# Two-level gates from the fourth token group on, with the sums of the gate weights made one group earlier

## The chip, the cores and the metric

The kernel runs on one core of one Trainium2 chip. The metric is the device time of one execution in microseconds. The kernel before took 752.95 us, the median of three runs between 752.68 and 754.04 us. Engines are called by the profile's names: PE is TensorE (PEld its weight loads), DVE is VectorE, ACT is ScalarE, POOL is GpSimd, and SP issues most DMAs.

## The reference

The computation is a linear attention followed by a multiplicative feed-forward block, all in 32-bit floats. There are 8 batches, 8 heads, 576 positions and head size 64, so 4608 tokens of width 512; the inner width is 1024.

```python
kv = np.einsum('bhsd,bhse->bhde', k, v)
out = np.einsum('bhsd,bhde->bhse', q, kv)
rms = np.sqrt(np.mean(out * out, axis=-1, keepdims=True) + 1e-06)
attn = out / rms * g_norm
x = attn.transpose(0, 2, 1, 3).reshape(4608, 512)
a = x @ w1
b = x @ w2
return ((a * b) @ w3) @ w_out
```

## The kernel before

**Stages.** The kernel first multiplies w3 by w_out once (lines 1288 to 1376). Then it works through nine groups of 512 tokens in the order T = 0 to 6, 8, 7. Groups 0 to 7 are the first 512 positions of each batch; group 8 holds the 64 left-over positions of all batches. "The third group" is T = 2, "the fourth" is T = 3. A group has two parts: the gates, which compute a * b, and the projection with the folded weights (`project`, for T = 0, or `project_twice`).

**One-level gates.** `gates(T, p, ...)` handles row block p of four. It calls `winograd` (line 692), a Strassen-Winograd scheme of seven products in place of eight. A product is four fp32 matmuls of a 128x128 weight block against 256 token columns; the profile counts two instructions for each. PSUM results of the products a11, s1, s2 and s3 are copied to SBUF by ACT under the names p1, p5, u2 and u3 (`keep`, line 712); a piece c21 is copied at line 834. The third product adds into p1's PSUM bank, so PE cannot start it before the copy p1 is done; the fourth stands in the same way behind p5. DVE adds the parts and multiplies the two halves (lines 836 to 840). Twice in each block `winograd` calls `between()`: after u2 and after c11. That runs a step of `steps(T + 1)`, the attention of the next batch.

**Two-level gates.** Groups in IN_TWO, before the change T = 4, 5, 6, 8 and 7, do block 2 first, then blocks 0 and 1 together in `gates_of_two` (line 925), then block 3. `gates_of_two` applies the scheme a second time inside each of the seven products: twice 49 products of 128x128 against 128 columns (line 953), 196 instructions in the profile's count. It needs inner sums of the activations (`sum_x`, lines 918 to 921, eight DVE subtractions at the group's start) and of the weights.

**Weight sums.** `prepare_w` (line 870) is a generator of seven pieces, one for each outer product. A piece is three DVE instructions of 128x256 (lines 875 to 877) and three stores to the DRAM tile w_l2, or six for the products s1, s2 and s4, whose plain blocks are stored too. `replace_a21` (line 884) replaces seven blocks in place and stores three of them. Before the change three pieces are made in T = 2 (one behind each of the blocks 0 to 2) and four in T = 3 (two behind each of the blocks 0 and 1); `replace_a21` runs in block 2 of T = 3, at its first `between()`. The stored blocks come back in five DMAs by `load_w`: three in the projection of the group before the two-level group, the others within its gates.

**Turning by DMA.** q and the normed attention output x must be transposed. `turn_by_dma` (line 280) does that in three steps: a copy that separates the 16-bit halves (lines 297 and 299), a transposing DMA on SP (line 301), and a copy that joins the halves (line 311). For batches up to 4 (prepared in groups up to T = 3) POOL makes the copies; batch 1 is an exception, for which ACT makes most of them. For batches over FIRST_OF_TWO (5 on) `turns_by_scalar` (line 526) puts ACT's copies into slots. A slot is a key (stage, name): when `keep` or another copy with that name has been issued in that stage, `run_slot` traces the slot's calls, with an edge that holds them behind that copy on ACT. `begin` makes the first copy and the DMA, `end` the copy back. Keys such as (0, 3) belong to `gates_of_two` (half, product), ("p3", "u2") to a one-level block, and ("proj", "u2") to the projection.

**Order of work.** PE, POOL and SP run in the order in which the program is traced. DVE and ACT are ordered by the compiler's scheduler, except for stretches set by hand (DVE from block 3 on through the projection). `tc.issue_after(x)` adds an edge that keeps what is traced inside it behind x on x's own engine. SP therefore issues every store, load and transpose in traced order; one that waits holds all behind it. The trace has DVE waiting in order too, whatever the order is that the scheduler chose.

**PSUM.** Five banks serve the products (`ps_mm`), three the attention (`ps_at`).

Of the kernel before, what the change touches and what calls it, by code (L numbers as in the profile page):

```python
# [22 lines left out]
def kernel(  # L23
# [38 lines left out]
    DF = w1.shape[1]  # L62
    NP = H // 2
    KF = DF // P
    FIRST_OF_TWO = 4
    NH = KF // 2
    J = 4
    G = J * P
# [15 lines left out]
    def bank(pool, tag):  # L84
        return pool.tile([P, 512], FP32, name=tag, tag=tag)


    loaded, copies, adds = {}, {}, {}
# [166 lines left out]
    def all_of(steps):  # L255
        for _ in steps:
            pass
# [63 lines left out]
    def attention(b):  # L321
# [56 lines left out]
        def norm(o_ps, dsts):  # L378
# [3 lines left out]
            for i in range(n):  # L382
                sq = work.tile([P, G], FP32, name=f"sq{0 if b > FIRST_OF_TWO else i}", bufs=1)[:, 0:w]
                nc.scalar.activation(sq, o_ps[i], AF.Square)  # L384
# [41 lines left out]
        def product_left():  # L426

            xn = st["left"] = work.tile([P, NP, 2, D], FP32, name="xn_left", bufs=1)

            o_ps = [bank(ps_at, "at"), bank(*((ps_at, "at") if b > FIRST_OF_TWO else (ps_mm, "mm")))]  # L430
            for r in range(NP):
# [82 lines left out]
    def batch(b):  # L514
        if b not in batches:
            batches[b] = attention(b)
        return batches[b]

    slots, stage = {}, [None]
# [6 lines left out]
    def turns_by_scalar(b):  # L526

        a, turning = batch(b), {}

        def at(key, *call):  # L530
            slots.setdefault(key, []).append(call)

        def begin(name, f, *args):
            turning[name] = f(*args, nc.scalar.copy)
            next(turning[name])
            if name[0] == "q":
                next(turning[name])
            elif name[2]:
                for r in range(2):
                    next(turning["x", name[1], r])  # L540

        def end(name):
            all_of(turning[name])
            if name[0] == "q" and name[1] != "left":
                batch(name[1]).load_ahead("q", name[2])

        for r in (2, 3):
            at((0, 0), begin, ("q", b, r), a.q_by_dma, r)
        if b % 2:
            at(("p2", "c21"), begin, ("q", "left"), a.q_left_by_dma)  # L550
            at((0, 3), end, ("q", "left"))
        at((0, 6), end, ("q", b, 2))
        at((1, 0), end, ("q", b, 3))
        for h, begins, ends in (
            (0, ((0, 3), (0, 3)), ((1, 3), (1, 3))),
            (1, (("p3", "p1"), ("p3", "p5")), (("p3", "c21"), ("proj", "p1"))),
        ):
            for r in range(2):
                at(begins[r], begin, ("x", h, r), a.x_part_by_dma, h, r)
                at(ends[r], end, ("x", h, r))  # L560
        if b + 1 < B:
            n = batch(b + 1)
            for r in range(2):
                at(("p3", "u2"), begin, ("q", b + 1, r), n.q_by_dma, r)
                at(("proj", ("u2", "u3")[r]), end, ("q", b + 1, r))

    def steps(b):

        a = batch(b)
        a.start()
        more = b + 1 < B
        fs, ends = ([[] for _ in range(8)] for _ in range(2))

        def turn(i, f, *args, next_group=False):

            t = []

            def begin():
                t.append(f(*args))
                next(t[0])
                next(t[0])

            fs[i].append((begin,))
            (to_end if next_group else ends[i + 1]).append((lambda: all_of(t[0]),))

        if to_end:

            ends[0] += [(lambda: nc.gpsimd.tensor_copy(tick, late["p5"][:, 0, 0:1]),), *to_end]
        to_end.clear()
        odd = b % 2
        by_scalar = b > FIRST_OF_TWO
        if b == 1:
            early.extend(a.q_two_by_dma(r) for r in (0, 1))
            q_first = list(early)
            fs[0].append((a.begin_kv, 0, 1))

            def end_first():  # L600
                for t in q_first:
                    with tc.issue_after(copies["kv"].ins):
                        next(t)
                    all_of(t)

            ends[1].append((end_first,))
        fs[1] += [(a.begin_kv, 2, 3), (a.finish, 0)]
        if b == 1:
            last = {}

            def begin(name, behind, f, *args):
                last[name] = f(*args)
                with tc.issue_after(copies[behind][-1].ins):
                    next(last[name])
                next(last[name])

            def end(name, behind):
                with tc.issue_after(copies[behind][-1].ins):
                    next(last[name], None)
                all_of(last[name])  # L620

            fs[2] += [(begin, f"q{r}", "u2", a.q_two_by_dma, r) for r in (2, 3)]
            fs[3] += [
                (begin, "x", "u3", a.x_by_dma, 0, nc.scalar.copy),
                (begin, "left", "u3", a.q_left_by_dma),
            ]
            ends[4] += [(end, "q2", "p1"), (end, "q3", "p5"), (end, "x", "u2")]
            ends[5].append((end, "left", "u3"))
        elif by_scalar:
            turns_by_scalar(b)  # L630
        else:
            turn(1, a.q_two_by_dma, 2, 3)
            turn(2, a.x_by_dma, 0)
            if odd:
                turn(1, a.q_left_by_dma)
        second = 5 if b == 1 else 4
        if more:
            fs[second].append((batch(b + 1).begin_kv, 0, 1))
        fs[second].append((a.finish, 1))
        if odd:  # L640
            fs[3 if by_scalar else second].append((a.product_left,))
        if b == 1:
            turn(6, a.x_by_dma, 1)
            turn(7, a.x_left_by_dma, next_group=True)
        else:
            if not by_scalar:
                turn(5, a.x_by_dma, 1)
            if odd:
                turn(5, a.x_left_by_dma, next_group=more)
        if more and not by_scalar:  # L650
            turn(7 if b == 1 else 5, batch(b + 1).q_two_by_dma, 0, 1, next_group=True)
        if more:
            fs[7 if odd else 0].append((load_q_left, b + 1))
        return iter([lambda s=e + f: [f(*args) for f, *args in s] for e, f in zip(ends, fs)])
# [229 lines left out]
    def replace_a21():  # L884
        for n, (name, _) in enumerate(PRODUCTS):
            a11, _, a21, _ = w_blocks(name)
            nc.vector.tensor_sub(a21, a11, a21)
            if (0, n, "s3") in BLOCKS:
                store_w(n, "s3", a21)
# [387 lines left out]
    TWICE = (B, B - 1)  # L1277
    IN_TWO = (*range(FIRST_OF_TWO, B - 1), *TWICE)

# [8 lines left out]
    with tc.manual_schedule(  # L1288
# [6 lines left out]
        for e in range(2):  # L1295
            nc.scalar.dma_start(
                out=g_row[:, e * D:(e + 1) * D], in_=g_norm.rearrange("(o d) -> o d", o=1)
# [85 lines left out]
    for n, T in enumerate(groups):  # L1383
        pieces = steps(T + 1) if n + 2 < NG else iter([])

        def between():
            if len(converted) < len(begun):
                with tc.issue_after(copies["u2"][-1].ins):
                    end_next()
            next(pieces, lambda: None)()  # L1390
            if T == 1:
                for _ in range(2):
                    if next(preparing, 0) == 0 and len(loaded_b) < 3:
                        load_b()
            if T == FIRST_OF_TWO - 1 and p == 2 and not replaced:
                replaced.append(True)
                replace_a21()

        if T in IN_TWO:
            p = 2  # L1400
            stage[0] = "p2"
            with tc.issue_after(adds["out"].ins):
                sum_x(T)
            gates(T, p, between)
            run(sum_ab(p))
            if T in TWICE:
                in_order = tc.manual_schedule(engines={mybir.EngineType.DVE})
                in_order.__enter__()
            gates_of_two(T, between)
            of_two = sum_ab_two()  # L1410
            for _ in range(2):
                of_two.pop(0)()
        for p in range(NF):
            if T in IN_TWO and p + 1 < NF:
                continue
            stage[0] = f"p{p}" if T in IN_TWO else None
            if T and p + 1 == NF:
                sum_1, sum_2, sum_4, sum_3 = sum_ab(p)
                following = {
# [50 lines left out]
            else:  # L1470
                ops = [step() for step in sum_ab(p)]
                with tc.issue_after(ops[-1].ins):
                    for _ in range({(2, 0): 1, (2, 1): 1, (2, 2): 1, (3, 0): 2, (3, 1): 2}.get((T, p), 0)):
                        next(preparing_w)
        last = n + 1 == NG
        if T:
            project_twice(
# [7 lines left out]
        preparing, preparing_w, replaced = prepare_b(), prepare_w(), []  # L1485
# [32 lines left out]
```

## Time and profile before

The profiled execution took 753.1 us; the span from its first to its last instruction is 751.3 us. The median of the three timed runs is 752.95 us.

| what | value |
|---|---|
| median of three runs | 752.95 us |
| profiled execution, its span | 753.1 us, 751.3 us |
| granted TensorE clock | 0.999 |
| projection of T = 2, of T = 3, of T = 4 | 21.89, 21.89, 21.88 us |
| whole group T = 2 (239.11 to 315.62) | 76.51 us |
| whole group T = 3 (315.62 to 391.69) | 76.07 us |
| whole group T = 4 (391.69 to 465.73) | 74.04 us |
| whole group T = 5 (465.73 to 538.89) | 73.16 us |
| line 868, stores of weight sums | 33 of 128 KB, landing 1.9 to 2.1 us after the issue (medians by source) |
| line 301, transposing DMAs | 66 |

The groups are cut where the PE timeline goes from line 1162 (projection) to line 699 (one-level gates). The odd batches have the left-over product at line 435 as well (prepared in T = 2 for batch 3, in T = 4 for batch 5), so an odd group is compared with an odd one. In a timeline a row gives start and length in us, the engine (a q marks its sequencer, which issues DMAs), the line, the operation with its tiles and shape, the number of instructions merged, and in brackets the idle time before it with what ended it.

### The profile page before, as it was taken

Reading aid. Unit: us, or ns where it says so; the run is one execution under the profiler, and the core shown is the slowest. Engines: PE = TensorE matmul, PEld = TensorE weight load, DVE = VectorE, ACT = ScalarE, POOL = GpSimd, SP = SyncE. Lnnn points to the kernel's source line nnn. Section 1 sums busy time; section 2 is a strip of 40 time slices with the busy share of each in tenths; the row PEclk is TensorE's granted clock in tenths of the full one; section 3 lists DMA queues with packets and bytes.
Section 4 is the critical chain, followed back from the end, with each engine's and each line's share of the span. In section 5 each row is a group of like instructions: output and inputs, shape, how many; then the busy total and the mean of one; then the engine's idle time right before and its main releaser. Section 6 shows DMA issues by size and latency. Waiting matters only on the chain.

```text
span 751.3 us, 15612 instructions
## 1 busy us (share of the span) xinstructions
PE 743.1 (99%) x6155; PEld 659.0 (88%) x6155; DVE 636.4 (85%) x1301; ACT 322.2 (43%) x558; POOL 84.6 (11%) x83
## 2 busy tenths in 40 slices
PE   7999999999999999999999999999999999999998
PEld 5455788888899889988999999999999999999997
DVE  6977999648889679877798899889979997899897
ACT  6687878313222332233225753565367323222321
POOL 0000000222520442044201000100001000000000
PEclk9999999999999999999999999999999999999999
DMA  9996955349997947697468986799658663465354
GB/s 306 327 349 193 280 147 118 88 73 280 330 300 264 242 138 207 231 245 217 134 240 228 246 274 225 221 256 259 239 148 208 213 221 108 150 221 177 126 199 140
DMA packets 155245, 160.94 MB, mean 214 GB/s; under 512 B 87076, under 2 KB 140068, under 8 KB 155172
## 3 DMA queue, kind: packets, MB, share of 16 engines
q1 hardware_dynamic: 152720, 145.52, 65.8%
q10 hardware_dynamic: 2452, 14.42, 5.6%
q8 instruction: 49, 0.80, 0.4%
q14 instruction: 24, 0.20, 0.1%
HBM read 121.90 MB, written 20.71 MB: 190 GB/s over the span
## 4 chain that ended last, share of the span: by engine, by line
PE 96%; DMA 2%; DVE 2%; ACT 1%; issue 0%; SPq 0%; ACTq 0%
PE mm L699 45%; PE mm L1162 23%; PE mm L953 15%; PE mm L678 7%; PE at L340 3%; PE at L416 2%; DMA raw<-in_moe_w_out_dram 1%; PE at L665 1%; DMA raw<-in_moe_w_dram 0%; PE at L1213 0%; PE at L435 0%; PE at L359 0%; DVE c L839 0%; DVE chunks L174 0%; DVE inv L385 0%; DVE raw L875 0%
## 5 line engine op out<-in xcount | busy, mean ns | idle before, releaser
L699 PE MATMUL mm<-xT,w_sb 128*128 128x256 f32 x576 | 132.2, 379 | 0.0
L699 PEld LDWEIGHTS mm<-xT,w_sb 128*128 128x128 f32 x576 | 108.7, 190 | 14.8 <-issue 0.5
L699 PE MATMUL mm<-xc,ws 128*128 128x256 f32 x416 | 94.8, 380 | 0.4 <-ACT p L712 0.4
L699 PEld LDWEIGHTS mm<-xc,ws 128*128 128x128 f32 x416 | 78.8, 190 | 12.1 <-ACT p L712 1.5
L678 PE MATMUL mm<-chunks,ab 128*128 128x512 f32 x128 | 60.2, 603 | 1.4 <-DVE chunks L174 1.0
L712 ACT COPY u<-mm 128x512 f32<-128x512 f32 x46 | 27.0, 587 | 74.3 <-PE mm L699 58.9
L712 ACT COPY p<-mm 128x512 f32<-128x512 f32 x54 | 31.5, 586 | 53.2 <-PE mm L699 40.5
L699 PE MATMUL mm<-xc,w_sb 128*128 128x256 f32 x208 | 50.0, 383 | 0.0
L1162 PE MATMUL mm<-w3o_sb,ab 128*128 128x128 f32 x368 | 48.6, 275 | 0.0
L1173 ACT COPY u<-mm 128x512 f32<-128x512 f32 x23 | 13.5, 586 | 81.6 <-DVE raw L1186 47.7
L1162 PE MATMUL mm<-w3o_sb,raw 128*128 128x128 f32 x372 | 48.1, 275 | 0.0
L699 PE MATMUL mm<-xT,ws 128*128 128x256 f32 x192 | 45.8, 381 | 0.0
L1162 PEld LDWEIGHTS mm<-w3o_sb,ab 128*128 128x128 f32 x368 | 45.4, 192 | 0.4
L1162 PEld LDWEIGHTS mm<-w3o_sb,raw 128*128 128x128 f32 x372 | 44.8, 192 | 0.0
L699 PEld LDWEIGHTS mm<-xc,w_sb 128*128 128x128 f32 x208 | 38.9, 190 | 5.5
L678 PEld LDWEIGHTS mm<-chunks,ab 128*128 128x128 f32 x128 | 21.8, 190 | 23.9 <-issue 15.3
L840 DVE TENSOR_TENSOR ab<-c 128x256 f32<-128x256 f32 x78 | 40.7, 522 | 2.1
L385 DVE TENSOR_REDUCE inv<-sq 128x8 f32<-128x512 f32 (+1 forms) x40 | 24.1, 627 | 20.9 <-ACT sq L384 20.6
L834 ACT COPY c<-mm 128x256 f32<-128x256 f32 x26 | 9.7, 372 | 72.6 <-PE mm L699 72.6
L699 PEld LDWEIGHTS mm<-xT,ws 128*128 128x128 f32 x192 | 36.1, 190 | 5.0
L953 PE MATMUL mm<-ws,w3o_sb 128*128 128x128 f32 x250 | 38.5, 275 | 0.0
L297 POOL COPY xT<-xn 128x1024 uint16<-128x1024 uint16 x14 | 17.1, 1249 | 151.5 <-DVE xn L394 151.5
(249 smaller groups left out, 1627.6 us busy)
## 6 DMA issues: line engine op xcount, KB each, us to landing
w3o_sb<-w3o_l SPq DMA_DIRECT2D x18, 896.0 KB, 5.3
raw<-in_moe_w_dram SPq DMA_DIRECT2D x31, 512.0 KB, 7.1
raw<-w3o_l SPq DMA_DIRECT2D x15, 896.0 KB, 4.8
w3o_sb<-w_l SPq DMA_DIRECT2D x15, 896.0 KB, 5.3
w3o_sb<-w3o_l ACTq DMA_DIRECT2D x14, 896.0 KB, 4.6
k_sb<-in_k_dram SPq DMA_DIRECT2D x32, 256.0 KB, 4.5
v_sb<-in_v_dram SPq DMA_DIRECT2D x32, 256.0 KB, 4.8
q_sb<-in_q_dram SPq DMA_DIRECT2D x32, 256.0 KB, 3.6
```

What stands on the lines that cost most here:

```text
L297: copy(to, src.rearrange("p a n w -> p w a n"))
L340: nc.tensor.matmul(kv_ps[e * D:(e + 1) * D, r - rs[0], :], lhsT=k_sb[:, e, cols] if j < J else kl[:, 2 * r + e, :], rhs=v_sb[:, e, cols] i ...
L385: nc.vector.tensor_reduce(out=inv[:, i], in_=sq.rearrange("p (h d) -> p h d", d=D), axis=AX.X, op=ALU.add)
L416: nc.tensor.matmul(o_ps[l][tokens, n * D:(n + 1) * D], lhsT=qT[r][rows, e, i, tokens], rhs=kv_b[rows, e, r, :], start=True, stop=True,)
L678: nc.tensor.matmul(sums_ps[half][m], lhsT=w3T[half, c][:, m, :], rhs=chunks[:, c, 1, :], start=(c == 0), stop=(c == KF - 1),)
L699: nc.tensor.matmul(ps[:, u, :], lhsT=lhsT(a_name, u, c), rhs=rhs(b_name, c),  start=(u == 0 and c == 0 and to is None), stop=(c == chunks ...
L712: copies.setdefault(name, []).append(nc.scalar.copy(t, ps))
L834: copied = nc.scalar.copy(c, one[:, 0, :])
L840: nc.vector.tensor_mul(dst, c[:, 0, :], c[:, 1, :])
L953: nc.tensor.matmul(ps[place // 4][:, place % 4, :], lhsT=x, rhs=y, start=new and place // 4 not in seen, stop=True, skip_group_check=True,)
L1162: nc.tensor.matmul(to[:, i, :], lhsT=x[:, c, :], rhs=y[:, c, :], start=new and place // 4 not in seen, stop=(c == 1), skip_group_check=True,)
L1173: nc.scalar.copy(t[:, 0:4], ps[0])
```

## The change

FIRST_OF_TWO goes from 4 to 3. With it the gates of T = 3 become two-level for blocks 0 and 1, and `turns_by_scalar` is used for batches from 3 on, so ACT makes the copies around the DMA turns in T = 2 and T = 3, where POOL made them. In T = 2 the gates are still one-level, with blocks in the order 0 to 3, and batch 3 gets slots of its own in that order: q of the pairs 2 and 3 begins behind p1 and p5 of block 1 and ends behind its u3; the left-over q begins behind c21 of block 0 and ends behind p5 of block 2; x of the first half begins behind u2 of block 1 and ends behind c21 of block 1 and p1 of block 2. The slots of block 3 and the projection are those of the later groups.

All seven pieces of `prepare_w` are now made in T = 2: two at the start of the group, behind the last DVE instruction of the projection before, two behind block 0 and three behind block 1. `replace_a21` runs at the second `between()` of block 2. `load_w` follows in the projection of T = 2.

```diff
-    FIRST_OF_TWO = 4
+    FIRST_OF_TWO = 3
...
+        if b > FIRST_OF_TWO:
+            q_begins, q_ends = ((0, 0), (0, 0)), ((0, 6), (1, 0))
+            left_q = ("p2", "c21"), (0, 3)
+            x_begins, x_ends = ((0, 3), (0, 3)), ((1, 3), (1, 3))
+        else:
+            q_begins, q_ends = (("p1", "p1"), ("p1", "p5")), (("p1", "u3"), ("p1", "u3"))
+            left_q = ("p0", "c21"), ("p2", "p5")
+            x_begins, x_ends = (("p1", "u2"), ("p1", "u2")), (("p1", "c21"), ("p2", "p1"))
         for r in (2, 3):
-            at((0, 0), begin, ("q", b, r), a.q_by_dma, r)
+            at(q_begins[r - 2], begin, ("q", b, r), a.q_by_dma, r)
         if b % 2:
-            at(("p2", "c21"), begin, ("q", "left"), a.q_left_by_dma)
-            at((0, 3), end, ("q", "left"))
-        at((0, 6), end, ("q", b, 2))
-        at((1, 0), end, ("q", b, 3))
+            at(left_q[0], begin, ("q", "left"), a.q_left_by_dma)
+            at(left_q[1], end, ("q", "left"))
+        for r in (2, 3):
+            at(q_ends[r - 2], end, ("q", b, r))
         for h, begins, ends in (
-            (0, ((0, 3), (0, 3)), ((1, 3), (1, 3))),
+            (0, x_begins, x_ends),
...
-        by_scalar = b > FIRST_OF_TWO
+        by_scalar, in_two = b >= FIRST_OF_TWO, b > FIRST_OF_TWO
...
-            fs[3 if by_scalar else second].append((a.product_left,))
+            fs[3 if in_two else second].append((a.product_left,))
...
-            if T == FIRST_OF_TWO - 1 and p == 2 and not replaced:
+            if T == FIRST_OF_TWO - 1 and p == 2:
                 replaced.append(True)
-                replace_a21()
+                if len(replaced) == 2:
+                    replace_a21()
...
+        def prepare_some(pieces):
+            if T == FIRST_OF_TWO - 1:
+                for _ in range(pieces):
+                    next(preparing_w)
+
+        if T == FIRST_OF_TWO - 1:
+            with tc.issue_after(adds["out"].ins):
+                prepare_some(2)
...
-            stage[0] = f"p{p}" if T in IN_TWO else None
+            stage[0] = f"p{p}" if T in IN_TWO or T == FIRST_OF_TWO - 1 else None
...
                 ops = [step() for step in sum_ab(p)]
                 with tc.issue_after(ops[-1].ins):
-                    for _ in range({(2, 0): 1, (2, 1): 1, (2, 2): 1, (3, 0): 2, (3, 1): 2}.get((T, p), 0)):
-                        next(preparing_w)
+                    prepare_some({0: 2, 1: 3}.get(p, 0))
```

## The prediction

> **What bounds the kernel now.** I number the groups by the program's T; the third group is T2, the fourth T3. I read the page first, then the busy times in stretches cut where the PE timeline changes from one group's gates to its projection.
>
> ```profile
> PE 743.1 (99%) x6155; PEld 659.0 (88%) x6155; DVE 636.4 (85%) x1301; ACT 322.2 (43%) x558; POOL 84.6 (11%) x83
> PE 96%; DMA 2%; DVE 2%; ACT 1%; issue 0%; SPq 0%; ACTq 0%
> ```
>
> TensorE is busy for 99% of the span and makes 96% of the chain that ended last. So only two things can move the time: TensorE's own work, and new gaps in it. A change on another engine counts only where it makes or closes such a gap.
>
> ```profile
> 239.11:293.73 54.62, 54.49 (x466) 47.45 (x465) 39.73 (x76) 16.11 (x36) 22.48 (x20) 1.00 0.74 187
> 315.62:369.80 54.18, 53.82 (x434) 46.86 (x433) 40.01 (x78) 15.06 (x33) 22.42 (x19) 1.00 0.75 200
> 391.69:443.85 52.16, 52.16 (x550) 48.41 (x549) 46.91 (x100) 31.89 (x56) 4.42 (x4) 1.00 0.91 245
> 465.73:517.00 51.27, 51.27 (x518) 47.71 (x517) 44.31 (x97) 29.50 (x51) 2.43 (x3) 1.00 0.90 254
> ```
>
> These are the gates of T2, T3, T4 and T5: length, then busy time of PE, PEld, DVE, ACT, POOL. T2 and T3 are one-level, T4 and T5 two-level for two of the four row blocks. T3 and T5 both work on an even batch ahead, so they differ by the form of the gates and by the engine of the turn copies.
>
> ```profile
> 332.04 1.89 PE L699 MATMUL mm<-xc,ws 128*128 128x256 f32 x8
> 334.29 1.99 PE L699 MATMUL mm<-xc,ws 128*128 128x256 f32 x8 [0.36 <-ACT p L712]
> 336.12 1.89 PE L699 MATMUL mm<-xT,ws 128*128 128x256 f32 x8
> ...
> 333.45 0.31 ACT L389 ACTIVATE inv<-inv,eps_col 128x16 f32<-128x16 f32 x1 [2.57 <-DVE inv L385]
> 333.67 1.05 ACT L712 COPY p<-mm 128x512 f32<-128x512 f32 x2
> ```
>
> This is T3's one stall. Sixteen matmuls took 4.08 us here (332.04 to 336.12), elsewhere 3.46. ScalarE stood in its square root, which waited for VectorE, and the PSUM copy p1 behind it came late; TensorE may not write that bank again before p1 is copied. The same chain decides what happens in T2 after the change.
>
> ```profile
> 253.97 4.44 SPq L301 DMA_TRANSPOSE q_sb<-qT  x2
> 258.50 1.26 SPq L301 DMA_TRANSPOSE ql_sb<-qT_left  x1
> 259.86 1.60 SPq L868 DMA_DIRECT2D w_l<-raw  x3
> ...
> 346.69 2.67 SPq L868 DMA_DIRECT2D w_l<-ws  x3
> ...
> 262.88 0.59 ACT L712 COPY u<-mm 128x512 f32<-128x512 f32 x1 [2.81 <-PE mm L699]
> 266.33 0.38 ACT L834 COPY c<-mm 128x256 f32<-128x256 f32 x1 [2.87 <-PE mm L699]
> 268.06 0.59 ACT L712 COPY p<-mm 128x512 f32<-128x512 f32 x1 [1.35 <-PE mm L699]
> ...
> DMA to landing us min/median/max: 2.7/3.0/6.5
> ```
>
> SP takes 1.26 us to issue a transposing DMA and about 0.53 us for each store of a weight sum; ScalarE has 1 to 3 us free between PSUM copies in T2. The last line is for all transposes (L301).
>
> **What the Trainium skill says.** (1) SBUF — State Buffer, "Who interferes with whom": a VectorE instruction with two SBUF inputs contends with a GpSimd instruction that reads SBUF, and the later one blocks. The trace agrees: the 128x256 subtraction of L875 took 1.25 us at 329.64, under a POOL copy, and that of L876 at 330.81 0.41. (2) Perfetto Trace Analysis, "Tensor Engine Instruction (MATMUL, LD_WEIGHTS)": ScalarE, VectorE and GpSimd run strictly in order. The p1 copy above agrees. (3) The same page, "DMA Instruction — HWDGE (DVE, Sync)": the issuing sequencer is held while descriptors are made, and the data moves outside the span shown. Here 0.5 us on SP, landing about 2 us after the issue. (4) TensorE: Matmul & The Clock Gate, "LDWEIGHTS": a load is paid by columns; its formula gives 107 ns for 128. The trace spaces 128-column matmuls by 112 ns, so narrow matmuls still just hide their loads.
>
> **The change part by part.** *T3's gates.* Row blocks 0 and 1 now take 2 x 7 x 8 = 112 matmul instructions of 256 columns; 16 take 3.455 us (317.35 to 320.80), 0.216 each: 24.2 us. Two-level they take 196 of 128 columns; 12 take 1.34 us (295.07 to 296.41), 0.1117 each: 21.9 us. That saves 2.3. T3 also loses its stall, 0.62, since what caused it (sums of weights under POOL copies in the square root's way) leaves the group. Sum 2.9; the stretches say the same, 54.18 - 51.27 = 2.91. What T3 gains in VectorE work (L918 to L921, 8 subtractions, and the L978 to L995 sums) is in T4 and T5 already and stalled nothing there. Five loads of w_l2 move from T3's projection and T4 to T2's projection and T3; in T4 they sat beside full TensorE work. The three load_b after T2's projection move to the end of T3's gates, where T4 has them (428.61 to 432.12, needed from 443.85). I cost all this at 0; if the loads lost their cover, one costs its 5.3 us to landing once.
>
> *T4.* Its opening POOL copies (396.24, 3.05 us) go to ScalarE as in T5. T5 plus product_left (0.72, the hole between 415.53 + 0.22 and 416.47) makes 51.99 against 52.16. I take 0.1.
>
> *T2, VectorE.* It gets 7 pieces of sums instead of 3 and the 7 subtractions of replace_a21: 12 + 7 = 19 more of 128x256, 0.42 us each, 8 us. VectorE was busy 39.7 of 54.6, and it loses most of the blocking by POOL (eight sums and products of 256 or 512 columns stood at 1.05 to 1.46 us instead of 0.42 to 0.69). The first two pieces start behind L1186 (243.01), partly under the POOL copies still there (243.54 to 245.8), and end near 247.5; c12's add, ready at 246.5, has no PSUM bank waiting on it soon, as the ring has five. Pieces 3 and 4 run near 252.2 to 254.4, before the reductions, as the single piece does now. Cost 0, between -0.2 (0.24 of stall near 244) and +0.6 (a repeat of T3's stall).
>
> *T2, SP and ScalarE.* Here I see the price. SP runs in traced order. Pieces 3 and 4 bring 6 + 6 stores, traced after block 0 and before block 1's slots, hence ahead of the transposes of q. On ScalarE the left-over q's copy follows c21 (254.24) and ends at 255.6; its transpose is issued 255.6 to 256.9; 12 stores at 0.52 end at 263.1; q r = 2 and r = 3 take 263.1 to 265.7, x the next 2.6. At the median landing of 3.0 from issue, q is there at 266.1 and 267.4. But their copies back are put behind u3 (262.88 + 0.59 = 263.5), so ScalarE waits, in order: r = 2 until 267.3, r = 3 until 268.6 (1.16 each, from L311), c21 until 269.0, x r = 0 (landed 268.7) until 270.05, then p1 of block 2 at 270.6. TensorE wants p1's bank at 269.6 (block 2 starts at 266.13, two products take 3.46). Loss 1.1. Behind p1 come x r = 1, p5 and left q by 273.2, in time for product_left near 274.8. If x r = 0 is queued behind p1, or the copies of q are queued later, the loss is 0; if landing takes 4.0 (340.53 to 344.52 behind nine stores) it is 2.1. I take 1.1 because every copy back in T4 and T5 stands directly behind its slot. Later stores (12 of pieces 5 to 7, 3 of replace_a21) hold back only loads for the next group; the turns in block 3 stand as in T4.
>
> *Sum.* -2.9 - 0.1 + 1.1 = -1.9. The profiled execution took 753.1 (span 751.3 plus 1.8 around it): 751.2. The median of the three runs, 752.95, is 0.15 lower, so I forecast 751.1.
>
> **The rivals.** *No stall in T2.* For it: ScalarE has 15 us of work in 54, and two waiting copies behind p1 would end it. Against: SP's arithmetic. Gives 752.95 - 3.0, or 750.0.
>
> *The gain is used up.* Landing 4 to 5 us behind the stores, as at 340.53 and at 182.84 (landed 188.3), gives 2.1 to 3.1 of loss in T2, or T3's kind of stall comes back beside it: 752.0 to 753.0, and to 754 if both do.
>
> *Slower: SP's queue.* One mechanism, the 12 stores in front of the transposes. At the pace of 346.69 (0.89 each) they end at 267.6; q r = 3 lands at 267.6 + 1.3 + 4.0 = 272.9, p1 ends 3.2 later, 276.1, and TensorE loses 6.5: 752.95 - 3.0 + 6.5, or 756.5. It decides from a loss of 4.5, that is when q r = 3 lands after 270.9, 3.5 later than I have it. For it: two transposes in T1 took 4.4 us each to issue (208.49, 212.93). Against: DMA was at 1.04 of its engines in T1, 0.74 in T2.
>
> **How the numbers follow.** Forecast (loss 0.6 to 1.6) 0.36: 750.6 to 751.6. No stall 0.24. Used up 0.24. Slower 0.16. Two tenths of a percent is 1.5 us, about what a measurement of this kernel tells from no change. Faster (below 751.45) takes the second case and most of the first, 0.55; same 0.29; slower 0.16. The range from 749.7 (no stall, T4 and the small gap near 244 gained too) to 754.3 leaves the slower case out. The forecast's own range, 750.6 to 751.6, stands beside it.
>
> **What would show it.** T3's gates near 51.3 with 196 L953 instructions (right) or over 52 (wrong). In T2's block 1, twelve L868 stores ahead of the two q transposes, those issued near 263; ScalarE idle before L311, ended by DMA q_sb<-qT; TensorE idle near 270, ended by ACT p L712. T2 at 55.7; at 54.6 the first rival holds, over 59 the third. It would be wrong in its base if T3 waited for w_l2 loads or if VectorE, not ScalarE, ended TensorE's waits in T2.

## The result and the profile after

The changed kernel takes 756.46 us, the median of six runs between 755.14 and 757.7. The kernel before takes 752.85 us beside it (six runs, 752.4 to 754.14). The ratio is 1.0044, with a 95% interval of 1.0029 to 1.0058: the change costs 3.6 us. The forecast was 751.1 us, the range 749.7 to 754.3.

The line numbers from `keep` on are 8 higher now: 699 became 707 (gates matmul), 712 became 720 (the PSUM copies p and u), 834 became 842 (c21), 868 became 876 (stores of sums). Lines 297 to 311 (the turns) stay.

From the page of the changed kernel, the busy times, the granted clock in 40 slices and the chain that ended last:

```profile
PE 742.7 (98%) x6239; PEld 661.1 (87%) x6239; DVE 640.1 (85%) x1339; ACT 358.8 (47%) x598; POOL 43.0 (6%) x48
...
PEclk9999999999999989999999999999999999999999
...
PE 95%; DMA 1%; DVE 1%; ACT 1%; issue 0%; SPq 0%; ACTq 0%
```

TensorE bounds the kernel as before. The copies have moved from POOL (84.6 to 43.0 us) to ScalarE (322.2 to 358.8). New is the 8 in the clock row, in the slice from 264.5 to 283.4 us. The gates of T2, T3 and T4 in the same view as before the change (length, busy time of PE, PEld, DVE, ACT and POOL, clock, DMA share, GB/s):

```profile
239.02:301.34 62.32, 56.72 (x466) 48.70 (x465) 41.84 (x95) 29.67 (x50) 4.14 (x4) 0.95 0.76 204
323.23:374.49 51.26, 51.26 (x518) 47.70 (x517) 43.57 (x95) 29.54 (x51) 2.25 (x3) 1.00 0.91 248
396.38:448.46 52.08, 52.08 (x550) 48.34 (x549) 45.67 (x102) 32.01 (x56) 1.04 (x1) 1.00 0.96 260
```

T2 took 7.70 us more than before (62.32 against 54.62), T3 2.92 less, T4 0.08 less. The sum is +4.7. The profiled execution took 757.7 us against 753.1, so these stretches hold the whole difference. (That execution was the slowest of the six; the medians differ by 3.6.)

T2's loss has one place. TensorE's timeline in block 2 of T2 (three dots mark rows left out):

```profile
267.64 1.89 PE L707 MATMUL mm<-xc,ws 128*128 128x256 f32 x8
275.04 3.78 PE L707 MATMUL mm<-xc,ws 128*128 128x256 f32 x8 [5.51 <-ACT p L720]
278.75 0.99 PE L340 MATMUL at<-v_sb,k_sb 128*64 128x64 f32 x16
...
281.62 0.27 PE L435 MATMUL at<-kv_sb,qT_left 64*64 64x64 f32 x1
```

The same place before the change, where the two products of eight follow each other without a gap:

```profile
267.86 3.62 PE L699 MATMUL mm<-xc,ws 128*128 128x256 f32 x16
...
274.01 0.24 PE L435 MATMUL at<-kv_sb,qT_left 64*64 64x64 f32 x1
```

After the change TensorE stood for 5.51 us until the copy p1 had freed its PSUM bank. Then eight matmuls took 3.71 us (275.04 to 278.75), where eight take 1.73 elsewhere. The changed kernel in stretches shows why:

```profile
269.50:272.60 3.10, 0.03 (x1) 0.00 (x0) 0.57 (x2) 2.32 (x3) 0.00 (x0) 1.00 0.91 205
272.60:275.00 2.40, 0.00 (x0) 0.00 (x0) 2.40 (x8) 1.65 (x3) 0.00 (x0) 0.51 0.80 220
275.00:279.40 4.40, 4.36 (x20) 3.14 (x22) 1.14 (x4) 3.08 (x4) 0.00 (x0) 0.50 1.02 296
```

The granted clock fell to half 3.1 us after TensorE had gone idle, and stayed there for 4.4 us of work. From the first of these matmuls to the left-over product (line 435) it took 6.58 us (275.04 to 281.62); the same stretch before the change took 4.42 (269.59, the middle of the sixteen, to 274.01). That is another 2.16 us. So 5.51 + 2.16 = 7.67 of T2's 7.70.

ScalarE at that place:

```profile
262.66 0.58 ACT L720 COPY u<-mm 128x512 f32<-128x512 f32 x1 [0.90 <-PE mm L707]
269.24 1.16 ACT L311 COPY qT<-q_sb 128x1024 uint16<-128x1024 uint16 x1 [5.99 <-DMA q_sb<-qT]
270.57 1.16 ACT L311 COPY qT<-q_sb 128x1024 uint16<-128x1024 uint16 x1 [0.18 <-DMA q_sb<-qT]
271.64 0.36 ACT L842 COPY c<-mm 128x256 f32<-128x256 f32 x1
273.35 1.16 ACT L311 COPY xT<-xn 128x1024 uint16<-128x1024 uint16 x1 [1.35 <-DMA xn<-xT]
274.41 0.58 ACT L720 COPY p<-mm 128x512 f32<-128x512 f32 x1
```

It was idle for 5.99 us in front of the copy back of q, and for 1.35 more in front of that of x. p1's copy, last line, was behind both. SP, which issues these DMAs:

```profile
243.63 3.56 SPq L876 DMA_DIRECT2D w_l<-raw  x3
...
248.44 0.44 SPq L876 DMA_DIRECT2D w_l<-raw  x1
248.97 2.85 SPq L97 DMA_DIRECT2D q_sb<-in_q_dram  x2
...
252.39 2.38 SPq L97 DMA_DIRECT2D v_sb<-in_v_dram  x1
...
257.31 2.57 SPq L301 DMA_TRANSPOSE ql_sb<-qT_left  x1
259.98 1.57 SPq L876 DMA_DIRECT2D w_l<-inner_sums  x3
...
264.81 1.57 SPq L876 DMA_DIRECT2D w_l<-ws  x3
266.48 2.58 SPq L301 DMA_TRANSPOSE q_sb<-qT  x2
269.17 2.60 SPq L301 DMA_TRANSPOSE xn<-xT  x2
```

The twelve stores of the third and fourth piece of weight sums begin at 259.98 and end at 266.4, and the transposes of q and x stand behind them. From 243.63 on SP has no pause of more than about 0.1 us.

The theory (A in the expectations): the place of stores on SP makes transposes late, ScalarE's copies back wait for them in order, the PSUM copy p1 waits behind these, TensorE behind p1, and its clock falls meanwhile. Its rivals: B, ScalarE has more to do in T2 than fits; C, VectorE's 19 more instructions in T2 make something late.

### The profile page after: what moved, and what is told of

It reads as the page before. It is cut to its first block, busy times and chain, and to the rows that moved or that the text cites. A ratio compares the mean times of both kernels' runs of the same rounds, so it can differ in the third digit from the quotient of the medians.

```text
span 755.8 us, 15827 instructions
## 1 busy us (share of the span) xinstructions
PE 742.7 (98%) x6239; PEld 661.1 (87%) x6239; DVE 640.1 (85%) x1339; ACT 358.8 (47%) x598; POOL 43.0 (6%) x48
## 4 chain that ended last, share of the span: by engine, by line
PE 95%; DMA 1%; DVE 1%; ACT 1%; issue 0%; SPq 0%; ACTq 0%
PE mm L707 41%; PE mm L1170 23%; PE mm L961 18%; PE mm L686 7%; PE at L340 3%; PE at L416 2%; PE at L673 1%; DMA raw<-in_moe_w_out_dram 1%; PE at L1221 0%; DMA xn<-xT 0%; DMA q_sb<-qT 0%; PE at L435 0%; ACT kv_sb L351 0%; DVE ab L164 0%; PE at L359 0%
## 5 line engine op out<-in xcount | busy, mean ns | idle before, releaser
L707 PE MATMUL mm<-xT,w_sb 128*128 128x256 f32 x528 | 121.2, 379 | 0.0
L707 PEld LDWEIGHTS mm<-xT,w_sb 128*128 128x128 f32 x528 | 99.5, 190 | 13.5 <-issue 0.5
L707 PE MATMUL mm<-xc,ws 128*128 128x256 f32 x384 | 89.2, 385 | 5.5 <-ACT p L720 5.5
L707 PEld LDWEIGHTS mm<-xc,ws 128*128 128x128 f32 x384 | 73.8, 193 | 16.7 <-ACT p L720 6.5
L720 ACT COPY u<-mm 128x512 f32<-128x512 f32 x42 | 24.6, 586 | 61.8 <-PE mm L707 51.3
L961 PE MATMUL mm<-ws,w3o_sb 128*128 128x128 f32 x300 | 46.2, 275 | 0.0
L707 PE MATMUL mm<-xc,w_sb 128*128 128x256 f32 x192 | 46.2, 383 | 0.0
L385 DVE TENSOR_REDUCE inv<-sq 128x8 f32<-128x512 f32 (+1 forms) x40 | 24.3, 628 | 23.3 <-ACT sq L384 23.2
L707 PE MATMUL mm<-xT,ws 128*128 128x256 f32 x176 | 41.9, 381 | 0.0
L707 PEld LDWEIGHTS mm<-xc,w_sb 128*128 128x128 f32 x192 | 35.8, 190 | 5.1
L961 PEld LDWEIGHTS mm<-ws,w3o_sb 128*128 128x128 f32 x300 | 39.8, 192 | 0.0
L848 DVE TENSOR_TENSOR ab<-c 128x256 f32<-128x256 f32 x72 | 34.2, 475 | 2.0
```

The costliest lines, as they stand in the source:

```text
L385: nc.vector.tensor_reduce(out=inv[:, i], in_=sq.rearrange("p (h d) -> p h d", d=D), axis=AX.X, op=ALU.add)
L707: nc.tensor.matmul(ps[:, u, :], lhsT=lhsT(a_name, u, c), rhs=rhs(b_name, c),  start=(u == 0 and c == 0 and to is None), stop=(c == chunks ...
L720: copies.setdefault(name, []).append(nc.scalar.copy(t, ps))
L848: nc.vector.tensor_mul(dst, c[:, 0, :], c[:, 1, :])
L961: nc.tensor.matmul(ps[place // 4][:, place % 4, :], lhsT=x, rhs=y, start=new and place // 4 not in seen, stop=True, skip_group_check=True,)
```

## The experiments

All are edits of the changed kernel, and all were timed beside the kernel before. The first column of the table is the time in us from T2's first matmul to the issue of the first of the two q transposes, from SP's timeline; the second is TensorE's wait for p1 in block 2; the third is the length of T2's gates. These three are read from one profiled execution of each kernel, the median and the ratio from all its timed runs.

| run | q transposes at | wait for p1 | T2's gates | median | ratio to before, 95% |
|---|---|---|---|---|---|
| the change | 27.5 | 5.51 | 62.32 | 756.46 | 1.0029 to 1.0058 |
| three early stores later | 25.6 | 3.52 | 59.77 | 755.37 | 1.0016 to 1.0037 |
| wait filled with matmuls | 26.7 | 4.77, filled | 59.48 | 754.66 | 1.0015 to 1.0033 |
| all copies back later | 25.7 | none | 58.07 | 753.40 | 0.9985 to 1.0007 |
| x copies back later | 26.0 | 1.69 | 57.91 | 752.84 | 0.9990 to 1.0006 |
| six stores later | 23.3 | 1.28 | 56.12 | 751.41 | 0.9968 to 0.9989 |
| POOL turns in T2 | 17.6 | none | 56.17 | 751.17 | 0.9969 to 0.9983 |
| twelve stores later | 19.2 | none | 54.34 | 749.79 | 0.9942 to 0.9969 |

T3's gates are 51.26 or 51.27 us in all eight kernels.

**Twelve stores later.** Only the place of twelve stores on SP changes; VectorE still makes every sum where it did.

```diff
-    def store_w(n, key, src):
+    held = []
+    def store_w(n, key, src, hold=False):
+        if hold:
+            held.append((n, key, src))
+            return
...
-                    store_w(n, key, t)
+                    store_w(n, key, t, n in (2, 3))
...
                 ops = [step() for step in sum_ab(p)]
+                while p == 1 and held:
+                    store_w(*held.pop(0))
                 with tc.issue_after(ops[-1].ins):
```

> The changed kernel with one edit: in the third group (T2) the twelve stores of the third and fourth piece's sums stand on SP behind the transposes of the second block, not ahead of them. VectorE and ScalarE get the same instructions in the same order. Theory A (SP's queue: the stores hold back the transposes of q and x, ScalarE's copies back of them hold back the PSUM copy p1): the q transposes are issued about 6.4 us earlier, near 260, q r = 3 lands near 264.3; TensorE's wait of 5.5 us in block 2 is at most 0.3, and its slow 2.2 us after it are gone; T2's gates go from 62.3 to about 54.5, the time to 749 to 750. Theory B (ScalarE has too much to do in T2 with the copies around DMA turns) and theory C (VectorE's 19 more instructions hold something back): nothing that they speak of changes, so T2 stays near 62 and the time near 756.5.

Measured: 749.79 us, ratio to before 0.9955. In this kernel SP's timeline has the transposes ahead of the stores (lines are 5 higher):

```profile
257.15 1.65 SPq L301 DMA_TRANSPOSE ql_sb<-qT_left  x1
258.89 2.61 SPq L301 DMA_TRANSPOSE q_sb<-qT  x2
262.38 2.59 SPq L301 DMA_TRANSPOSE xn<-xT  x2
...
266.40 1.48 SPq L881 DMA_DIRECT2D w_l<-inner_sums  x3
```

ScalarE's timeline has the same copies in the same order, without waits for a DMA:

```profile
263.73 2.23 ACT L311 COPY qT<-q_sb 128x1024 uint16<-128x1024 uint16 x2
266.70 0.37 ACT L842 COPY c<-mm 128x256 f32<-128x256 f32 x1 [0.75 <-PE mm L707]
266.97 1.16 ACT L311 COPY xT<-xn 128x1024 uint16<-128x1024 uint16 x1
268.43 0.58 ACT L720 COPY p<-mm 128x512 f32<-128x512 f32 x1 [0.30 <-PE mm L707]
```

p1 now waits for TensorE, not TensorE for p1. The stretch of T2's gates:

```profile
239.72:294.06 54.34, 54.26 (x467) 47.51 (x466) 40.28 (x93) 29.68 (x50) 4.05 (x4) 1.00 0.86 233
```

T2 takes 54.34 us, less than before the change (54.62). B and C are out: ScalarE has the same 50 instructions here as in the change, VectorE 93 of its 95 with all of the added sums among them, and nothing of it stalls TensorE. The transposes come 8.3 us earlier than in the profile of the change; 6.4 are the stores, the rest is that SP was less late ahead of them. This version is also faster than both kernels.

**Six stores later: half the dose.** The same edit with `n == 3` in place of `n in (2, 3)`.

> The changed kernel with only the six stores of the fourth piece's sums behind the transposes of the second block: half the dose. Theory A: the transposes come 6 x 0.535 = 3.2 us earlier; TensorE's wait in block 2 falls from 5.5 to about 2.3 us, too short for the slow stretch behind it, so T2's gates take about 57 and the time is near 752 (751.3 to 752.7). If the clock falls after any gap of 2 us, another 1 to 2 us are lost. Theories B and C: T2 near 62, the time near 756.5.

Measured: 751.41 us, T2 56.12. From the list of TensorE's waits:

```profile
PE mm L707 <- ACT p L720: 1.3, 1, 1.3
```

The q transposes were issued 23.3 us into T2, 4.1 earlier than in the change (3.2 for six stores, the rest because SP was less late ahead of them in this execution), and the wait fell by 4.2. In the profile of the run of three early stores below the two differ from the change by 1.9 and 2.0. That makes a slope of one in this range: each microsecond by which the transposes are late is one on TensorE. The clock stayed at 1.00.

**POOL turns in T2.** POOL makes the copies around the turns of batch 3 again; two-level gates and the place of the sums stay.

```diff
-        by_scalar, in_two = b >= FIRST_OF_TWO, b > FIRST_OF_TWO
+        by_scalar, in_two = b > FIRST_OF_TWO, b > FIRST_OF_TWO
```

> The changed kernel with POOL, not ScalarE, making the copies around DMA turns in T2; the two-level gates of the fourth group and all sums of weights in the third stay. The stores stay ahead of the transposes on SP. Theory A: the transposes land as late as before, but POOL waits for them and no PSUM copy stands behind it, so TensorE's wait of 5.5 us is gone; T2 takes 54.5 to 56 (POOL's copies block VectorE again) and the time is 750 to 751.5. Theory B: the wait goes too. Theory C (VectorE): T2 gets worse than 62, since VectorE has its 19 more instructions and POOL's blocking as well.

Measured: 751.17 us, T2 56.17. My expectation had one thing wrong: this edit also moves the begin of q's turn, so that its transposes were issued ahead of the stores (256.33), and only those of x behind them (268.76). So the run doesn't separate A from B. It shows where late transposes hurt if POOL makes the copies. The four rows are from the timelines of POOL, VectorE, ScalarE and TensorE:

```profile
275.73 2.24 POOL L311 COPY xT<-xn 128x1024 uint16<-128x1024 uint16 x2 [8.23 <-DMA xn<-xT]
...
278.00 1.29 DVE L394 TENSOR_TENSOR xn<-at,inv 128x512 f32<-128x512 f32 x2 [2.07 <-DMA w_l<-ws]
...
279.65 0.30 ACT L389 ACTIVATE inv<-inv,eps_col 128x8 f32<-128x8 f32 x1 [3.74 <-DVE inv L385]
...
280.94 1.99 PE L707 MATMUL mm<-xc,w_sb 128*128 128x256 f32 x8 [1.40 <-ACT u L720]
```

POOL waited 8.23 us for the x transposes. Its copies read xn until 277.97, and there is one xn; VectorE's next write to xn begins at 278.00. (The profile names a DMA as releaser; the POOL copy that ends 0.03 us ahead, with the one buffer, fits better.) ScalarE's square root waited for VectorE, the copy u for ScalarE, TensorE for u. On SP the x transposes stand behind the twelve stores here too; that moving these would end the stall was not tried.

**Wait filled with matmuls.** Added work that no output uses: 22 matmuls ahead of the product that waits for p1, in block 2 of T2 only.

```diff
         p5 = keep("p5", r2)
+        if fill[0]:
+            t = bank(ps_at, "at")
+            for _ in range(fill[0]):
+                nc.tensor.matmul(t[:, 0:P], lhsT=ident, rhs=ident, start=True, stop=True)
         product("s2", "t2", r1)
...
+            fill[0] = 22 if (T, p) == (2, 2) else 0
             gates(T, p, between if T or p else lambda: None)
```

> The changed kernel with 22 more matmuls of 128 columns of the identity, into a bank of their own, in block 2 of T2 just ahead of the matmuls that wait for p1; nothing reads them (added work, about 22 x 0.112 to 0.22 = 2.5 to 4.9 us inside the wait). It measures the slow stretch by itself. If the 2.2 us lost behind the wait come from TensorE standing idle[...], the wait ends at the same time, the matmuls behind it run at full pace at once, T2's gates take about 60.2 and the time is 754.3 to 755.5. If the slow stretch has another cause, T2 stays at 62.3 and the time near 756.5.

Measured: 754.66 us, T2 59.48. TensorE's timeline, with the fill in the second row (the profile counts two instructions for each matmul):

```profile
267.28 1.89 PE L707 MATMUL mm<-xc,ws 128*128 128x256 f32 x8
269.01 5.07 PE L732 MATMUL at<-ident 128*128 128x128 f32 x44
273.94 1.99 PE L707 MATMUL mm<-xc,ws 128*128 128x256 f32 x8
275.86 0.69 PE L340 MATMUL at<-v_sb,k_sb 128*64 128x64 f32 x16
```

The copy p1 ended at 273.88 here, and the matmuls behind the fill go on at once at full pace (1.92 us for eight to the next row, against 3.71). The transposes were 0.8 us earlier than in the profile of the change, which takes 0.74 off the wait; the other 2.1 of T2's 2.84 less is the clock. So the slow stretch comes from TensorE standing idle, and the clock's part is shown by itself.

**x copies back later.** ScalarE makes the copies of x behind p1 and p5 of block 2. SP's order is unchanged.

```diff
-            x_begins, x_ends = (("p1", "u2"), ("p1", "u2")), (("p1", "c21"), ("p2", "p1"))
+            x_begins, x_ends = (("p1", "u2"), ("p1", "u2")), (("p2", "p1"), ("p2", "p5"))
```

> The changed kernel with one edit: in T2, ScalarE's copies back of x stand behind the PSUM copies p1 and p5 of block 2, not ahead of p1. All DMAs are issued in the same order as in the changed kernel. Theory A (ScalarE stands in its order behind copies that wait for late transposes): the copy of x r = 0 no longer stands ahead of p1, and it waited there for the second x transpose, since both turns are staged in the one tile that it writes. p1 can start behind c21, about 2.4 us earlier (272.0 instead of 274.41); TensorE's wait falls from 5.5 to about 3.1 us, T2 takes 57.8 if the clock then holds and up to 59.9 if it still falls, the time is 752.0 to 754.1. If it is TensorE's or VectorE's own work that is late, nothing changes: 756.5.

Measured: 752.84 us, T2 57.91. TensorE's waits:

```profile
PE mm L707 <- ACT p L720: 1.7, 1, 1.7
PE at L435 <- ACT kv_sb L351: 1.7, 1, 1.7
```

The wait for p1 fell by 3.8: 2.4 are the edit's, as expected, and 1.4 came from transposes that were issued earlier in this execution. A second wait appeared: the copies of x now stand ahead of those of kv_sb, and the left-over product waits for them. That wait was not in the expectation; it was in the next one.

**All copies back later.**

```diff
-            q_begins, q_ends = (("p1", "p1"), ("p1", "p5")), (("p1", "u3"), ("p1", "u3"))
+            q_begins, q_ends = (("p1", "p1"), ("p1", "p5")), (("p2", "p1"), ("p2", "p5"))
...
-            x_begins, x_ends = (("p1", "u2"), ("p1", "u2")), (("p1", "c21"), ("p2", "p1"))
+            x_begins, x_ends = (("p1", "u2"), ("p1", "u2")), (("p2", "u2"), ("p2", "u2"))
```

> The changed kernel with all copies back of q (r = 2 behind p1, r = 3 behind p5) and of x (behind u2) one block later on ScalarE; the DMAs on SP stay as late as they are. Theory A: p1 is on time, TensorE's wait of 5.5 us and the slow stretch behind it are gone. What is late next: p5 behind the copy of q r = 2 (about 0.5 us), and the copies of kv_sb behind those of x (about 2.9 us), so T2 takes 55 to 58 and the time is 749.8 to 752.5. If late data of q and x themselves hold up TensorE, not the copies' place in ScalarE's order, the wait only moves and stays near 5.5 us: 756.

Measured: 753.40 us, 0.9 above the range expected; T2 58.07. The wait for p1 is gone although the q transposes were still issued 25.7 us into T2, where the run with 25.6 has a wait of 3.52. So it was the copies' place in ScalarE's order that held TensorE, not the data. The wait for kv_sb is there with 2.25 us (2.9 expected). The missing part is the clock, in stretches:

```profile
274.10:276.30 2.20, 0.03 (x4) 0.00 (x0) 0.00 (x0) 2.17 (x6) 0.00 (x0) 1.00 0.53 149
276.30:279.60 3.30, 3.23 (x37) 2.75 (x38) 2.50 (x6) 2.07 (x6) 0.00 (x0) 0.51 0.87 222
```

A gap of 2.2 us was enough for 3.3 us at half clock, which cost about 1.6. I had taken it to be too short.

**Three early stores later.** The stores edit with `n == 1`: three stores at the group's start go behind the transposes.

> The changed kernel with the three stores of the second piece's sums, at the start of T2's gates, moved behind the transposes of the second block; the twelve stores of the third and fourth piece stay ahead of them. It asks why the twelve begin at 260.0 and not at 256.9, as predicted. If SP is simply full from the group's start (the stores of the first two pieces push the loads of q, k and v, these the transpose of the left q), taking three stores of 0.53 us out moves the twelve and the transposes 1.6 us forward, TensorE's wait falls to about 3.9 us, T2 takes about 60.5 and the time is 754 to 755 (752.5 if the clock no longer falls). If the loads or the left q set the time by themselves, the twelve still begin at 260 and the time stays near 756.5.

Measured: 755.37 us, T2 59.77, wait 3.52. SP's timeline:

```profile
243.46 3.56 SPq L881 DMA_DIRECT2D w_l<-raw  x3
247.12 1.02 SPq L97 DMA_DIRECT2D q_sb<-in_q_dram  x2
...
252.86 0.62 SPq L107 DMA_DIRECT2D vl_sb<-in_v_dram  x1
256.39 1.28 SPq L301 DMA_TRANSPOSE ql_sb<-qT_left  x1
257.76 1.58 SPq L881 DMA_DIRECT2D w_l<-inner_sums  x3
```

The left q's transpose starts when its copy on ScalarE is done, after 2.9 us in which SP issued nothing, and takes 1.28 us; the twelve begin 19.0 us into T2 instead of 21.0. In the change SP was so late that this pause was gone. How much of the two microseconds the three stores cost is not shown, though: with all six early stores in place the twelve began 19.2 us into T2 in the run with all copies back later, 19.5 in that with the x copies later and 20.2 in that with the filled wait, and the intervals of this run and of the change overlap. T2 is 0.7 us below what was expected and the median 0.4 above its range; the profile that I reckoned from was the slowest execution of the change. The clock fell after the gap of 3.52 us as well: the eight matmuls behind it took 3.34 us.

## Why the prediction went wrong

*What bounds the kernel, T3 and T4* were right: T3's gates take 51.26 us (forecast 51.3), T4's 52.08 (52.06). *VectorE in T2*, costed at 0, was right too: with the stores moved, its 19 more instructions leave T2 at 54.34.

*T2, SP and ScalarE* is the step that failed. It named the mechanism, each of its links, and the place: TensorE waiting for p1 in block 2. Its loss of 1.1 us was mis-sized; the profiled execution lost 7.67.

| link | predicted, us | measured, us |
|---|---|---|
| left q's transpose issued | 256.9 | 259.88 |
| twelve stores end | 263.1 | 266.4 |
| q r = 3 landed | 267.4 | 270.55 |
| copy of x r = 0 begins | 269.0 | 273.35 |
| copy p1 ends | 270.6 | 274.99 |
| TensorE wants the bank | 269.6 | 269.5 |
| slow clock behind the wait | not counted | 2.16 |

The first link on ScalarE in the change, where the left q's copy (L299) stands behind a square root (L389):

```profile
255.28 0.31 ACT L389 ACTIVATE inv<-inv,eps_col 128x16 f32<-128x16 f32 x1 [0.88 <-DVE inv L385]
255.50 1.03 ACT L299 COPY qT_left<-ql_sb 128x1024 uint16<-128x1024 uint16 x1
```

- *SP's start, 3.1 us.* Three things add up before the twelve stores begin. The prediction let the left q's copy on ScalarE follow c21 at once and end at 255.6. ScalarE's square root, which waits for VectorE, stood between, so the copy ended at 256.53, 0.9 later (rows above). Then, the prediction placed the first two pieces on VectorE at the group's start and didn't count their six stores on SP. These held SP until 248.9, the loads behind them ended at 257.2 instead of 253.9 in the kernel before, and the transpose began at 257.31, 0.8 after its copy. Last, its issue took 2.57 us, not 1.26: 1.3 more. A transpose right behind the loads was slow before the change too: of the 4.44 us of the two at 253.97, in the prediction's own lines, the first took 3.09 and the second 1.25.
- *The pace and the landing* were nearly right: 0.535 us for a store (0.52 predicted), 2.74 from issue to landing (3.0).
- *The copy of x, 1.35 us.* The prediction let it start once its own transpose had landed. It started at the landing of the second one. In `x_part_by_dma` both turns are staged in the halves of the one tile xT, and the copy back of r = 0 writes into both halves; so it must wait until the second transpose has read its half. This is read from the code and the trace; no run stages the two turns apart. It cost 1.35 us in the profile of the change and 1.30, 1.35 and 1.37 in three experiments that keep the order of the copies.
- *The clock, 2.16 us.* Not in the sum at all. The Trainium skill, TensorE: Matmul & The Clock Gate, "What's actually happening", says that the array is gated to 4/8, half its clock, after an idle window of about 3.4 us and needs about as long a busy one to come back; here the fall came 3.1 us into the gap. A loss of 1.1 us would not have called for it; the bound of the landing at 4.0 us, 2.1 of loss, comes near what the runs show to be enough.

Of the rivals, the slower one (SP's queue) has the right sign, the right mechanism, and with 756.5 us the median almost to the digit; that its price agrees is partly luck. It had stores at 0.89 us and a landing of 4.0, neither of which came; it had TensorE lose 6.5 by waiting alone. Measured, q r = 3 landed at 270.55, not at its 272.9, and just ahead of 270.9, the point from which the prediction called the change slower. The wait for x and the clock, which no case had, carried the time beyond.

Two readings in the prediction are a little off and decide nothing: with its own 1.16 us the copy of x r = 0 would end at 270.16, not 270.05; and of the two transposes at 182.84 one landed 2.9 us after its issue, the other 5.5, with loads of k and v directly ahead of them.

SP's lateness varies from profile to profile. With the same instructions ahead on SP, the q transposes were issued 25.7, 26.0, 26.7 and 27.5 us into T2 in four kernels, one execution each. That fits the six times of the change, spread over 2.6 us; why some issues take longer was not settled.

## What to carry to other kernels

When a step moves, write out the queue of its DMA issuer and that of the engine that feeds it, from the group's start, before pricing what stands behind them: here twelve stores of half a microsecond ahead of four transposes turned a gain of 3.4 us (749.79 against 753.17 beside it) into a loss of 3.6. ScalarE, which ran in order here and made both the PSUM copies and the copies back of DMA turns, passed the latest transpose on to TensorE; check there what each copy really waits for, its staging included. A TensorE gap of 2.25 us or more had a second price in the clock, so a loss can grow faster than the lateness that makes it.

## What the runs showed of the hardware

The clock fell to half after shorter gaps than I had thought. Gaps of 1.28 and twice 1.69 us left it at 1.00; 2.25 us brought 3.4 us at half clock, 3.52 brought the eight matmuls behind it to 3.34 us, 5.51 took 4.4 us of work at half clock. From the begin of the gap to the fall it was 2.2 to 3.1 us. The same page of the Trainium skill advises, under "Why this matters for your kernels", against gaps over about 3 us; the gap of 2.25 us differs from that, and the measurement decides. The page, under "What's actually happening", calls the window free-running, and the traces fit that. The clock stayed at half from 272.64 to 279.47 in the change, from 272.36 to 275.78 in the run of three early stores and from 276.35 to 279.77 with all copies back later: 6.83, 3.41 and 3.41 us, so twice or once the same length. Counted back by that length from each fall, TensorE had stood idle for 3.1, 3.0 and 2.2 us of 3.41; a part of the window was enough. The work just ahead of the gap of 2.25 us was also narrower, matmuls of 64 columns; whether that counts, no run tells.

The issue of one DMA on SP is not a constant. The first load of v in T2 took 0.47 us on SP in the run of twelve stores later and 2.38 in the change; the second took 1.86 and 0.46. The left q's transpose took 2.17 to 2.57 us when SP came to it within 0.1 us of the last load, 1.64 to 1.96 after a pause of 0.5 to 1.1, and 1.28 after one of 2.9 (seven profiles). What makes it so was not tested.
